# First head of clustered attention: its stack and its row of maxima written by the engines instead of by transfers

## The chip, the cores and the metric

The kernel runs on one core of a Trainium2 chip. The core has five engines that work side by side: TensorE (PE, matrix products, with weight loads as PEld), VectorE (DVE), ScalarE (ACT), GpSimd (POOL) and SyncE (SP), which here only starts transfers. Each has its own queue of instructions in a fixed order, and they wait for each other by semaphores. Matrix products land in PSUM; everything else lies in SBUF, which has 128 partitions. The metric is the device time in microseconds.

## The reference

Clustered attention over 2 batches of 8 heads, 768 positions, width 64, and then two expert layers.

```
q_assign = argmax(q_n @ c_n.T);  k_assign = argmax(k_n @ c_n.T)     # 16 clusters a head
mask   = q_assign[..., :, None] == k_assign[..., None, :]
scores = where(mask, q @ k.T / 8, -1e9)
attn   = softmax(scores);  x = attn @ v            # x: 1536 x 512
h = x @ w_in;  x = (h - tanh(h)) @ w_out           # d_ff 2048
x = (sigmoid(x @ w_gate) * (x @ w_val)) @ w_out2   # d_ff 1536
```

## The kernel before, in words

The 16 heads are worked in 8 pairs. `pair_prep(s)` prepares pair s: it loads q and k (L489, two transfers each, 192 KB a transfer), turns them on PE (L499) and copies them from PSUM with ACT into `xtq` and `xtk` (L503), 128 rows of which 64 belong to each head. DVE rounds these to a high part in `hlq` and `hlk` (L508), and POOL makes the low part (L515). PE scores all positions against the clusters (L527, 12 products); DVE makes a one-hot of the winner in five steps (L539 to L549); PE turns the one-hots (L561, six transposes); ACT scales them into `oht` (L567): -2^100 times the one-hot for q, one minus the one-hot for k.

A head's operands lie in a "stack" `stk` of four planes of 128 rows: the q and k rows in partitions 0 to 63, the 16 one-hot rows in 64 to 79, parts of the low products above, and in row 96 of plane 2 the negated row maxima. An engine writes a partition only from the same partition of its source (or, out of PSUM, from the one that PE put it in), so all stack rows are written by transfers from SBUF to SBUF (`copy`, L240), started by SP in `part` (L578).

`head_max(h)` multiplies the stack's planes 0 and 1 (L633, two products a tile of 128 positions, six tiles a head) and DVE takes each row's maximum (L637); the six columns of maxima are turned by PE (L641), copied by DVE into `mt` (L643), and written by a transfer into row 96. `head_attend(h)` multiplies the stacks again with all rows (L668, L669), ACT takes the exponential twice (L672, in f32 and f16), POOL or DVE makes the f16 remainder (L682), and PE multiplies with v (L699 to L701). v's scale for each batch comes from maxima that DVE takes over loaded parts of v (`v_part`, L436), held in buffers of kind `pt`, and from a short chain (L453 to L458). The expert layers follow (L969, L1288), with weights loaded, split and multiplied group by group.

Two things set the order. Every piece of work is a task with a priority, and `Planner.run` puts the tasks into each engine's queue before the kernel is built, from its own table of costs and from the numbers in `PRM`. And 170 tasks of two idle products each (`keep_busy`, L418), with the lowest priority, fill PE's queue wherever the planner sees it with nothing to do at the start. All 340 products are always issued.

Of the kernel before, what the change touches and what calls it, by code (L numbers as in the profile page):

```python
# [26 lines left out]
PRM = dict(  # L27
    QUEUE=2.5, AH_PE=0.15, AH_ACT=0.316, AH_DVE=0.0, AH_POOL=0.697, AH_SP=1.315, N_BUSY=170, NR=2, NRH=1,
    HX=['hx', 'hhxx'], WAR=0.797, LM=11, LV=8, ZP1=-12.75, ZP=1.744, FD=0.173, FO=0.68, LOQ=0, VHI=0, VL=6.0,
    VLS=2.185, VR=17.353, ZSV=-18.475, ZRAW=12.924, ZT=1.25, ZH=13.805, ZHL=14.25, ZS=4.5, ZC=-11.964,  # L30
    ZOT=-36.883, ZD=11.75, ZDH=6.0, ZDM=7.0, ZVL=25.5, ZVS=49.843, ZX=-0.998, ZE=34.058, ZLOW=39.356,
    ZLOWP=2.75, SEMS=1.0, TC=0.456, TW=0.74, M2=1, ZQK=0.25, ZMS=-28.375, Z0=53.342, HB=94, NB4=5, ROWS=0.0155,
    VB=9.164, RAWL=2.2, NMID=2, NPL2=2, W1L=0.7, D1L=0.322, W2L=1.623, D2L=-0.754, ZI=7.032, ZJ=1.1)


class Task:
# [168 lines left out]
def tile_cluster_attention_moe(  # L205
# [266 lines left out]
    xt_done = {}  # L472
    last = {}

    def pair_prep(s):


# [58 lines left out]
        def scores():  # L536
            return at(sm)[:, 0:G * C].rearrange("p (g c) -> p g c", c=C)
# [34 lines left out]
        for hh in range(2):  # L572
            sk = Slot("stk")
            hd = 2 * s + hh
            stk[hd] = sk
            r = hh * D

            def part(n, f, dep, src, take=(), sk=sk, z=z, hh=hh, more=0):  # L578
                x = add(SP, DMA_C, z + PRM["ZD"] + PRM["ZDH"] * hh + more, f, dep, take, lat=n * ROWS)
                use(src, x)  # L580
                return x

            def hi(nm, r=r):
# [5 lines left out]
            ts = [part(64, lambda sk=sk, hi=hi: copy(at(sk)[0:64, 0], hi("q")), [hi_t["q"]], hl["q"], [sk])]  # L589
            ts.append(part(128, lambda sk=sk, hi=hi: copy(  # L590
                at(sk)[0:64, 1::2], hi("k").unsqueeze(1).to_broadcast([64, 2, S])), [hi_t["k"], ts[0]], hl["k"]))
            for x in range(2):
                ts.append(part(C, lambda sk=sk, x=x, hh=hh: copy(
                    at(sk)[64:64 + C, x], at(oht)[(2 * x + hh) * C:(2 * x + hh + 1) * C]), [m6, ts[0]], oht))
            mready[hd] = list(ts)
# [5 lines left out]
            ts.append(part(64, lambda sk=sk, lo=lo: copy(at(sk)[0:64, 2], lo("q")), lo_t["q"] + ts[:1], hl["q"], more=PRM["ZDM"]))  # L601
# [19 lines left out]
    def head_max(h):  # L621
# [863 lines left out]
```

## Time and profile before

| | |
|---|---|
| median of 3 timed runs | 801.94 us (801.39 to 802.08) |
| profiled execution, its own time | 801.26 us |
| its span | 799.3 us |
| PE busy | 779.2 us, 97% |
| DVE busy | 573.3 us, 72% |
| ACT busy | 439.4 us, 55% |
| POOL busy | 567.3 us, 71% |
| mean granted clock of PE | 0.993 |

Busy time of PE includes the idle products of L418. An engine with a low share is not the bound of the whole, but it can be the bound of a stage; so the stages at the start are read one by one below. The granted clock is 1.00 at 2.4 GHz and 0.50 at 1.2 GHz.

### The profile page before, as it was taken

The page shows a single profiled execution, that of the slowest core. Times are in us where ns is not written, and L with a number is a line of the kernel's source. Part 1 is how long each engine was busy: PE and PEld are TensorE (multiplying, and loading weights), DVE is VectorE, ACT ScalarE, POOL GpSimd, SP SyncE. Part 2 cuts the span into 40 slices and gives each one's busy share as a digit, 9 for nine tenths or more (in the row PEclk, how much of TensorE's full clock was granted, in tenths as well). Part 3 has the DMA queues.
Part 4 walks back from the last instruction along what each step waited for, and adds up shares of the span by engine and source line. Part 5 has one row for each costly group of instructions (what it writes and reads, how often), then busy time and mean ns, then how long its engine had stood idle before and what let it go on. Part 6 is the DMA issues. An engine that isn't in the chain of part 4 may idle for free.

```text
span 799.3 us, 15929 instructions
## 1 busy us (share of the span) xinstructions
PE 779.2 (97%) x5979; PEld 731.4 (92%) x5979; DVE 573.3 (72%) x1076; ACT 439.4 (55%) x852; POOL 567.3 (71%) x597
## 2 busy tenths in 40 slices
PE   8989999999899999999999999999999999999998
PEld 8879898888779998999999999998998999999996
DVE  4887887797997866987676686998267676676434
ACT  4176778878778635554445445646552625445240
POOL 4266778776879896788688787989495766757231
PEclk9998999999999999999999999999999999999999
DMA  8866665566353100321121232122112222121004
GB/s 189 209 175 134 146 159 123 132 152 154 89 148 113 62 1 1 107 93 56 57 100 41 66 93 80 64 80 84 38 53 80 80 79 80 44 84 46 0 1 159
DMA packets 69341, 72.95 MB, mean 91 GB/s; under 512 B 30256, under 2 KB 52880, under 8 KB 69264
## 3 DMA queue, kind: packets, MB, share of 16 engines
q1 hardware_dynamic: 69264, 71.93, 32.7%
q8 instruction: 47, 0.77, 0.4%
q14 instruction: 30, 0.25, 0.1%
HBM read 48.27 MB, written 3.15 MB: 64 GB/s over the span
## 4 chain that ended last, share of the span: by engine, by line
PE 77%; DVE 10%; POOL 3%; issue 3%; DMA 3%; ACT 2%; SPq 1%; DVEq 0%; POOLq 0%; ACTq 0%
PE over_left L969 16%; PE over_left L1288 14%; PE sm L1288 11%; PE sm L969 9%; PE over_right L969 5%; PE over_right L1288 4%; DVE finr L637 2%; PE sm L418 2%; PE sm L699 2%; PE sm L700 2%; PE sm L701 2%; PE bb L633 1%; DVE vs L614 1%; PE ba L668 1%; PE bc L633 1%
## 5 line engine op out<-in xcount | busy, mean ns | idle before, releaser
L682 POOL TENSOR_TENSOR pt<-pf,pt 128x768 f16<-128x768 f32 x45 | 77.5, 1736 | 34.3 <-ACT pt L672 18.5
L682 POOL TENSOR_TENSOR ptt<-pf,ptt 128x768 f16<-128x768 f32 x34 | 58.2, 1717 | 19.7 <-ACT ptt L672 15.6
L996 POOL TENSOR_TENSOR stk<-pf,hlq 128x384 fp32r<-128x384 f32 x25 | 26.1, 1045 | 33.2 <-ACT hlq L995 33.2
L637 DVE TENSOR_REDUCE finr<-bc 128x1 fp32r<-128x768 f32 x35 | 33.2, 950 | 15.6 <-PE bc L633 13.4
L699 PE MATMUL sm<-vs,pt 128*128 128x65 f16 x330 | 43.7, 196 | 0.4 <-DVE mt L643 0.4
L700 PE MATMUL sm<-vs,pt 128*128 128x64 f16 x330 | 43.3, 197 | 0.0
L701 PE MATMUL sm<-vs,pt 128*128 128x65 f16 x330 | 43.0, 193 | 0.0
L969 PE MATMUL over_left<-stk,w 128*128 128x384 f32 x158 | 40.1, 335 | 0.0
L1288 PE MATMUL over_left<-xh,stk 128*128 128x384 f32 x132 | 40.0, 335 | 0.0
L637 DVE TENSOR_REDUCE finr<-bb 128x1 fp32r<-128x768 f32 x35 | 33.2, 949 | 7.6 <-PE bb L633 7.5
L995 ACT ACTIVATE stk<-pf 128x384 fp32r<-128x384 f32 x41 | 21.4, 523 | 30.5 <-POOL pf L1318 11.6
L699 PEld LDWEIGHTS <-pt 128*128 128x128 f16 x330 | 31.2, 97 | 6.2 <-issue 6.0
L672 ACT ACTIVATE pf<-ba 128x768 f32<-128x768 f32 x35 | 28.8, 823 | 13.3 <-PE ba L669 11.4
L1308 DVE TENSOR_TENSOR pf<-over_left,pf 128x384 f32<-128x384 f32 x32 | 17.7, 553 | 25.2 <-ACT pf L1304 11.4
L969 PE MATMUL over_left<-w,stk 128*128 128x512 f32 x118 | 34.9, 392 | 0.0
L700 PE MATMUL sm<-vs,ptt 128*128 128x64 f16 x246 | 34.8, 197 | 0.0
L699 PE MATMUL sm<-vs,ptt 128*128 128x65 f16 x246 | 34.7, 195 | 0.0
L701 PE MATMUL sm<-vs,ptt 128*128 128x65 f16 x246 | 34.4, 194 | 0.0
L672 ACT ACTIVATE pf<-bc 128x768 f32<-128x768 f32 x30 | 24.8, 826 | 14.9 <-PE bc L669 12.4
L996 POOL TENSOR_TENSOR oht<-pf,stk 128x384 fp32r<-128x384 f32 x25 | 25.6, 1025 | 9.9 <-ACT stk L995 9.2
L700 PEld LDWEIGHTS <-pt 128*128 128x128 f16 x330 | 31.5, 98 | 0.6 <-issue 0.5
L701 PEld LDWEIGHTS <-pt 128*128 128x128 f16 x330 | 31.7, 100 | 0.0
(570 smaller groups left out, 3166.8 us busy)
## 6 DMA issues: line engine op xcount, KB each, us to landing
vs<-in_moe_w_out_dram SPq DMA_DIRECT2D x48, 256.0 KB, 2.4
stk<-hlq SPq DMA_DIRECT2D x32, 192.0 KB, 2.7
stk<-hlk SPq DMA_DIRECT2D x16, 384.0 KB, 5.4
vs<-in_moe_w_in_dram SPq DMA_DIRECT2D x24, 256.0 KB, 2.6
vs<-in_moe_w_gate_dram SPq DMA_DIRECT2D x24, 256.0 KB, 2.7
vs<-in_moe_w_val_dram SPq DMA_DIRECT2D x24, 256.0 KB
rawq<-in_q_dram SPq DMA_DIRECT2D x16, 192.0 KB, 4.9
rawk<-in_k_dram SPq DMA_DIRECT2D x16, 192.0 KB, 4.6
```

The lines of the kernel that those rows point to most:

```text
L418: nc.tensor.matmul(tiles["sm", 1][:, 0:P], busy, busy, start=True, stop=True)
L637: rd.append(use(mx, add(DVE, c_dve(S), z + t, lambda t=t, mx=mx: nc.vector.tensor_reduce(at(mh)[:, t:t + 1], at(mx)[:, :, 0:HALF], axis=AX ...
L672: nc.scalar.activation(o.rearrange("p (j n) -> p j n", j=2), at(st)[:, :, 0:HALF], AF.Exp, scale=scale)
L682: lambda nce=nc.vector if on_v else nc.gpsimd, pf=pf, pt=pt: nce.tensor_tensor(at(pt)[:, 1], at(pf), at(pt)[:, 0], op=ALU.subtract), [e0, e1])
L699: nc.tensor.matmul(oview()[:, t], ph, vv[:, 0:D + 1], start=(kt == 0), stop=False)
L700: nc.tensor.matmul(oview()[:, t, 0:D], ph, vv[:, D + 1:2 * D + 1], start=False, stop=False)
L701: nc.tensor.matmul(oview()[:, t], plo, vv[:, 0:D + 1], start=False, stop=(kt == T - 1))
L969: nc.tensor.matmul(ps, a, b, start=(i == 0), stop=(i == n - 1))
L995: a = add(ACT, c_acts(CH), z, lambda: nc.scalar.activation(hi(), src(), AF.Copy), deps, take)
L996: b = add(POOL, c_pool(CH), z, lambda: nc.gpsimd.tensor_tensor(lo(), src(), hi(), op=ALU.subtract), [a])
L1288: nc.tensor.matmul(at(bank[to])[:, 0:CH], lh, rh, start=start and i == 0, stop=stop and i == 3 * KH - 1, skip_group_check=True)
L1308: return use(x, use(bank[n], add(DVE, c_dve(CH), rank[0], lambda: nc.vector.tensor_tensor(at(x), ps(n), at(x), op=ALU.add), deps)))
```

## The change

For head 0 alone, six transfers go: q and k rows, the two times 16 one-hot rows, the low q rows and the row of maxima. ACT copies q and k from `xtq` and `xtk` straight into partitions 0 to 63 of the stack, since head 0's rows lie there already. The one-hots of pair 0 are written into a zeroed buffer `pad` (one of kind `pt`) at a column offset, so that a transpose of 80 columns puts the wanted 16 rows in PSUM partitions 64 to 79; ACT (for q) and DVE (for k) scale them from there into the stack. The maxima of head 0 are written into the same buffer behind 96 zero columns, so that a transpose of 97 columns puts a tile's maxima in PSUM partition 96; ACT copies that row into the stack, in two halves. The banks' release (`ramp`) follows the new tasks. Of `PRM` four numbers differ.

```diff
-    VLS=2.185, VR=17.353, ...
+    VLS=2.185, VR=15.055, ...
-    VB=9.164, RAWL=2.2, ... W2L=1.623, ...
+    VB=9.164, RAWL=2.354, ... W2L=1.842, ... ZL0=1.3, ...
...
+    t_pad = use(pad, add(DVE, 0.9, -40, lambda: nc.vector.memset(at(pad).bitcast(F32), 0.0), take=[pad]))
+    def first_stack(sk, xts, ev, m4, z):
+        ts = []
+        for x, nm in enumerate("qk"):
+            ts.append(use(xts[nm], add(ACT, c_act(S), z + PRM["ZL0"], lambda x=x, nm=nm: nc.scalar.activation(
+                at(sk)[0:64, x], at(xts[nm])[0:64], AF.Copy), ev[nm] + ts[:1], [sk] if x == 0 else [])))
+        for x in range(2):
+            sm = Slot("smr")
+            def rows_t(x=x, sm=sm):
+                for t in range(T):
+                    nc.tensor.transpose(at(sm).bitcast(BF16)[0:64 + C, t * P:(t + 1) * P],
+                                        pad_oh()[:, t, 2 * C * x:2 * C * x + 64 + C], ident16)
+            a = use(pad, add(PE, 0.5, z + PRM["ZOT"] - 1 + 0.1 * x, rows_t, [m4], [sm]))
+            src = lambda sm=sm: at(sm).bitcast(BF16)[64:64 + C, 0:S]
+            if x == 0:
+                b = add(ACT, c_act(S) + 0.1, z + PRM["ZOT"] - 1, lambda src=src: nc.scalar.activation(
+                    at(sk)[64:64 + C, 0], src(), AF.Copy, scale=-BIG), [a, ts[0]])
+            else:
+                b = add(DVE, c_dve(S), z + PRM["ZOT"] - 1, lambda src=src: nc.vector.tensor_scalar(
+                    at(sk)[64:64 + C, 1], src(), -1.0, 1.0, op0=ALU.mult, op1=ALU.add), [a, ts[0]])
...
+            if hd == 0:
+                ts = first_stack(sk, xts, ev, m4, z)
+                ts.append(use(xts["k"], add(ACT, c_act(S), z + PRM["ZL0"] + 6, lambda sk=sk: nc.scalar.activation(
+                    at(sk)[0:64, 3], at(xts["k"])[0:64], AF.Copy), ts[:1])))
+                ts.append(add(ACT, c_act(S), z + PRM["ZL0"] + 6, lambda sk=sk: nc.scalar.activation(
+                    at(sk)[0:64, 2], at(hl["q"])[0:64, 1], AF.Copy), lo_t["q"] + ts[:1]))
+                mready[hd] = ts[:4]
...
+        if h == 0:
+            out_t = []
+            for half in range(2):
+                sm = Slot("smr")
+                def tr(half=half, sm=sm):
+                    for j in range(3):
+                        t = 3 * half + j
+                        nc.tensor.transpose(at(sm)[0:97, j * P:(j + 1) * P], pad_max()[:, t:t + 97], ident)
+                c = use(mh, add(PE, 0.33, z + T + PRM["ZMS"], tr, rd, [sm]))
+                out_t.append(use(sm, add(ACT, c_act(HALF), z + T + PRM["ZMS"], lambda half=half, sm=sm: nc.scalar.activation(
+                    at(sk)[96:97, 2, half * HALF:(half + 1) * HALF], at(sm)[96:97, 0:HALF], AF.Copy), [c])))
+            ramp.extend(out_t)
+            return out_t
```

The planner then orders everything anew. Lines of the new kernel are shifted: L499 becomes L537, L527 L565, L561 L611, L633 L697, L637 L701, L539 to L549 L577 to L599.

SP's queue at the start, before; `stk_86` is the stack of head 0, `stk_87` of head 1, `pt` holds parts of v, and the second rawk is that of pair 1:

```order
L434 DMA pt_96<-in_v_dram 128x2x384
L434 DMA pt_97<-in_v_dram 128x2x384
L489 DMA rawq_120<-in_q_dram 128x6x64 x2
L240 DMA stk_86<-hlq_122 64x768
L489 DMA rawk_123<-in_k_dram 128x6x64 x2
L240 DMA stk_87<-hlq_122 64x768
L240 DMA stk_86<-hlk_125 64x2x768
```

And now:

```order
L434 DMA pt_97<-in_v_dram 128x2x384
L527 DMA rawq_120<-in_q_dram 128x6x64 x2
L527 DMA rawk_123<-in_k_dram 128x6x64 x2
L240 DMA stk_87<-hlq_122 64x768
L240 DMA stk_86<-hlq_122 32x768
L240 DMA stk_86<-hlk_125 32x768
```

One v load and head 0's transfer of q rows no longer stand ahead of pair 1's k load.

DVE's queue in the middle of the start, around the maxima chain of pair 2, before; `finr_113` holds the maxima of head 2 and `finr_114` those of head 3, `ptt` and `pt` parts of v, `mm` the pair's cluster maxima:

```order
L637 TENSOR_REDUCE finr_113<-bc_620 128x1
L539 TENSOR_REDUCE mm_126<-sm_71 128x24
L614 SCALAR_TENSOR_TENSOR vs_89<-rawv_92,sv,vs_89 128x6x64
L643 CAST mt_115<-sm_72 6x128
L541 TENSOR_TENSOR sm_71<-sm_71,mm_126 128x384
L436 TENSOR_REDUCE vm<-ptt_104 128x1
L543 TENSOR_TENSOR sm_71<-sm_71,first 128x384
L637 TENSOR_REDUCE finr_114<-bb_80 128x1
```

And now, where `finr_114` is head 2's:

```order
L701 TENSOR_REDUCE finr_114<-bc_621 128x1
L674 SCALAR_TENSOR_TENSOR vs_89<-rawv_92,sv,vs_89 128x6x64 x2
L436 TENSOR_REDUCE vm<-ptt_104 128x1
L722 CAST mt_116<-sm_71 6x128
L436 TENSOR_REDUCE vm<-ptt_105 128x1
L436 TENSOR_REDUCE vm<-ptt_106 128x1
L577 TENSOR_REDUCE mm_126<-sm_72 128x24
L453 TENSOR_REDUCE vm<-vm 128x1
L579 TENSOR_TENSOR sm_72<-sm_72,mm_126 128x384
```

Three reductions of v now stand in one piece ahead of pair 2's chain, and head 3's maxima behind it.

PE's queue between pair 1's k transposes and the first maximum of head 0, now (`pt_96` is `pad`, `ba_76` the first bank of maxima):

```order
L537 MATMUL smr_84<-ident,rawk_123 128x128 x3
L537 MATMUL smr_85<-ident,rawk_123 128x128 x3
L498 MATMUL sm_71<-ident_141,pt_96 80x128
L498 MATMUL smr_84<-ident_141,pt_96 80x128
L611 MATMUL smr_85<-ident_141,pt_96 64x128
L565 MATMUL sm_71<-cb,xtq_121 128x96
L697 MATMUL ba_76<-stk_86 128x384 x2
```

The one-hot transposes of pair 0 (six of each kind) stand behind pair 1's k transposes; before, L561 stood ahead of them.

## Rows read from the trace of the kernel before

**Rows 1.** The page: span, and busy time, share and instructions of each engine.

```profile
span 799.3 us, 15929 instructions
PE 779.2 (97%) x5979; PEld 731.4 (92%) x5979; DVE 573.3 (72%) x1076; ACT 439.4 (55%) x852; POOL 567.3 (71%) x597
```

**Rows 2.** Windows: length; busy PE, PEld, DVE, ACT, POOL; granted clock; DMA share, GB/s.

```profile
10.00:20.00 10.00, 8.74 (x117) 8.24 (x117) 5.00 (x8) 2.73 (x5) 2.02 (x3) 1.00 0.99 177
...
50.00:60.00 10.00, 7.60 (x38) 5.48 (x37) 9.84 (x15) 6.56 (x9) 5.03 (x4) 0.85 0.70 187
60.00:70.00 10.00, 10.00 (x130) 8.92 (x129) 7.93 (x14) 5.32 (x8) 7.49 (x5) 0.64 0.83 164
...
80.00:90.00 10.00, 8.43 (x73) 7.79 (x72) 8.41 (x14) 7.66 (x12) 6.04 (x4) 1.00 0.82 166
```

**Rows 3.** The chain that ended last, 9 to 24: start, us, what.

```profile
10.47 7.62 DMA rawk<-in_k_dram
```

**Rows 4.** Timeline of PE, 15 to 47: start, us, instructions, [idle before, releaser].

```profile
15.91 0.52 PE L561 MATMUL smr<-ident,oh 128*64 128x128 bf16 x6
16.37 0.96 PE L418 MATMUL sm<-busy 128*128 128x128 bf16 x14
18.22 0.52 PE L499 MATMUL smr<-ident,rawk 128*128 128x128 f32 x3 [0.90 <-DMA rawk<-in_k_dram]
18.57 0.49 PE L499 MATMUL sm<-ident,rawk 128*128 128x128 f32 x3
...
19.91 0.41 PE L527 MATMUL smr<-cb,xtq 128*128 128x96 f32 x2
...
22.56 0.60 PE L633 MATMUL ba<-stk 80*128 80x384 f32 x2
22.99 0.52 PE L633 MATMUL bb<-stk 80*128 80x384 f32 x2
...
36.94 0.42 PE L668 MATMUL bc<-stk 112*128 112x384 f32 x1
...
46.74 0.36 PE L527 MATMUL sm<-cb,xtq 128*128 128x96 f32 x2
```

**Rows 5.** Timeline of PE, 52 to 59.

```profile
52.78 0.51 PE L633 MATMUL bb<-stk 80*128 80x384 f32 x2
53.71 0.62 PE L633 MATMUL ba<-stk 80*128 80x384 f32 x2 [0.41 <-ACT ptt L672]
55.11 0.45 PE L668 MATMUL bc<-stk 112*128 112x384 f32 x1 [0.79 <-ACT pt L672]
...
56.77 0.80 PE L633 MATMUL bb<-stk 80*128 80x384 f32 x2 [0.67 <-DVE finr L637]
58.09 0.69 PE L668 MATMUL ba<-stk 112*128 112x384 f32 x1 [0.53 <-DVE finr L637]
```

**Rows 6.** Windows around the low clock, columns as in rows 2.

```profile
53.50:57.00 3.50, 1.84 (x7) 1.19 (x8) 3.50 (x7) 2.37 (x5) 1.65 (x1) 1.00 0.36 99
...
58.50:67.00 8.50, 8.50 (x83) 7.22 (x83) 6.67 (x11) 4.45 (x7) 5.91 (x5) 0.50 1.04 219
```

**Rows 7.** Timeline of ACT, 14 to 39.

```profile
14.52 0.87 ACT L503 ACTIVATE xtq<-smr 128x384 f32<-128x384 f32 x2 [5.45 <-PE smr L499]
...
30.00 0.99 ACT L567 ACTIVATE oht<-smr,row_b,row_w 64x768 fp32r<-64x768 bf16 x1 [10.30 <-PE smr L561]
...
37.93 0.81 ACT L672 ACTIVATE pf<-bc 128x768 f32<-128x768 f32 x1 [0.89 <-PE bc L669]
```

**Rows 8.** Timeline of DVE, 11 to 23.

```profile
11.49 0.95 DVE L436 TENSOR_REDUCE vm<-pt 128x1 f32<-128x768 f32 x1 [0.15 <-DMA pt<-in_v_dram]
...
22.88 0.56 DVE L539 TENSOR_REDUCE mm<-smr 128x24 f32<-128x384 f32 x1 [7.59 <-PE smr L527]
```

**Rows 9.** Chain, 46 to 60, and DMA issues, 0 to 70 (KB, us to landing).

```profile
47.14 4.70 DMA stk<-oht
...
stk<-hlk SPq DMA_DIRECT2D x5, 384.0 KB, 6.6
```

More of the change, by code (lines that the diff above doesn't have):

```diff
@@ L29 @@
     HX=['hx', 'hhxx'], WAR=0.797, LM=11, LV=8, ZP1=-12.75, ZP=1.744, FD=0.173, FO=0.68, LOQ=0, VHI=0, VL=6.0,
[L30 removed]
+    VLS=2.185, VR=15.055, ZSV=-18.475, ZRAW=12.924, ZT=1.25, ZH=13.805, ZHL=14.25, ZS=4.5, ZC=-11.964,
     ZOT=-36.883, ZD=11.75, ZDH=6.0, ZDM=7.0, ZVL=25.5, ZVS=49.843, ZX=-0.998, ZE=34.058, ZLOW=39.356,
     ZLOWP=2.75, SEMS=1.0, TC=0.456, TW=0.74, M2=1, ZQK=0.25, ZMS=-28.375, Z0=53.342, HB=94, NB4=5, ROWS=0.0155,
[L33 removed]
+    VB=9.164, RAWL=2.354, NMID=2, NPL2=2, W1L=0.7, D1L=0.322, W2L=1.842, D2L=-0.754, ZI=7.032, ZL0=1.3, ZJ=1.1)
 class Task:
@@ L473, in tile_cluster_attention_moe, with pad_oh, pad_max @@
     last = {}
+    pad = Slot("pt")
+    def pad_oh():
+        return at(pad).bitcast(BF16).rearrange("p a n -> p (a n)")[:, 0:T * P].rearrange("p (t c) -> p t c", c=P)
+    def pad_max():
+        return at(pad).bitcast(F32).rearrange("p a n -> p (a n)")[:, T * P // 2:T * P // 2 + 96 + T]
+    t_pad = use(pad, add(DVE, 0.9, -40, lambda: nc.vector.memset(at(pad).bitcast(F32), 0.0), take=[pad]))
[18 more added lines that the diff above has]
+                    at(sk)[64:64 + C, 1], src(), -1.0, 1.0, op0=ALU.mult, op1=ALU.add), [a, ts[0]])
+            ts.append(use(sm, b))
+            ramp.append(b)
+        return ts
     def pair_prep(s):
@@ L546, in pair_prep, with oh_v @@
             at(mm)[:, 1, :, 0], scores(), axis=AX.X, op=ALU.max), [m2])
+        if s == 0:
+            oh = pad
+        def oh_v(t):
+            return pad_oh()[:, t, 2 * D - 4 * C:] if s == 0 else at(oh)[:, t].rearrange("p x h c -> p (x h c)")
         def onehot():
+            if s == 0:
+                nc.vector.tensor_tensor(
+                    pad_oh()[:, :, 2 * D - 4 * C:].rearrange("p t (g c) -> p t g c", c=C),
+                    scores().rearrange("p (t g) c -> p t g c", t=T),
+                    at(mm)[:, 1].rearrange("p (t g) c -> p t g c", t=T).to_broadcast([P, T, G // T, C]), op=ALU.is_equal)
+                return
             nc.vector.tensor_tensor(at(oh).rearrange("p t x h c -> p (t x h) c"), scores(),
                                     at(mm)[:, 1].to_broadcast([P, G, C]), op=ALU.is_equal)
-        m4 = add(DVE, c_dve(G * C), z + PRM["ZC"] + 1, onehot, [m3], [oh])
+        m4 = add(DVE, c_dve(G * C), z + PRM["ZC"] + 1, onehot, [m3, t_pad] if s == 0 else [m3], [] if s == 0 else [oh])
         use(sm, m4)
@@ L587, in lo @@
                 return at(hl[nm])[r:r + 64, 1]
[L589 to L595, printed above, removed]
+            if hd == 0:
[4 more added lines that the diff above has]
+                    at(sk)[0:64, 2], at(hl["q"])[0:64, 1], AF.Copy), lo_t["q"] + ts[:1]))
+                use(hl["q"], ts[-1])
+                mready[hd] = ts[:4]
+            else:
+                ts = [part(64, lambda sk=sk, hi=hi: copy(at(sk)[0:64, 0], hi("q")), [hi_t["q"]], hl["q"], [sk])]
+                ts.append(part(128, lambda sk=sk, hi=hi: copy(
+                    at(sk)[0:64, 1::2], hi("k").unsqueeze(1).to_broadcast([64, 2, S])), [hi_t["k"], ts[0]], hl["k"]))
+                for x in range(2):
+                    ts.append(part(C, lambda sk=sk, x=x, hh=hh: copy(
+                        at(sk)[64:64 + C, x], at(oht)[(2 * x + hh) * C:(2 * x + hh + 1) * C]), [m6, ts[0]], oht))
+                mready[hd] = list(ts)
             for w, top in ((0, 64 + C), (1, 64)):
@@ L600, in pair_prep @@
                     at(sk)[top:top + 32, 2 * w + 1], lo("k")[32 * w:32 * w + 32]), lo_t["k"] + ts[:1], hl["k"], more=PRM["ZDM"]))
-            ts.append(part(64, lambda sk=sk, lo=lo: copy(at(sk)[0:64, 2], lo("q")), lo_t["q"] + ts[:1], hl["q"], more=PRM["ZDM"]))
+            if hd:
+                ts.append(part(64, lambda sk=sk, lo=lo: copy(at(sk)[0:64, 2], lo("q")), lo_t["q"] + ts[:1], hl["q"], more=PRM["ZDM"]))
             mrow[hd] = ts
@@ L625, in head_max, with mh_v @@
         sk = stk[h]
-        mh, mt, sm = Slot("finr"), Slot("mt"), Slot("smr" if h < NRH else "sm")
+        mh, mt, sm = pad if h == 0 else Slot("finr"), Slot("mt"), Slot("smr" if h < NRH else "sm")
         rd = []
+        def mh_v(t):
+            return pad_max()[:, 96 + t:97 + t] if h == 0 else at(mh)[:, t:t + 1]
         for t in range(T):
@@ L637, in head_max @@
             rd.append(use(mx, add(DVE, c_dve(S), z + t, lambda t=t, mx=mx: nc.vector.tensor_reduce(
-                at(mh)[:, t:t + 1], at(mx)[:, :, 0:HALF], axis=AX.XY, op=ALU.max, negate=True),
-                [a] + rd[:1], [mh] if t == 0 else [])))
+                mh_v(t), at(mx)[:, :, 0:HALF], axis=AX.XY, op=ALU.max, negate=True),
+                [a] + rd[:1], [mh] if t == 0 and h else [])))
         last["max"] = last.get("max", []) + rd
+        if h == 0:
[11 more added lines that the diff above has]
+            return out_t
         c = use(mh, add(PE, 0.11, z + T + PRM["ZMS"], lambda: nc.tensor.transpose(
```

3 lines of the change are left out of this document (1 added, 2 removed).

## The prediction, made before the changed kernel was run

> **What bounds the kernel now.** I read the page first. The span is 799.3 us and TensorE (PE) is busy 97% of it [rows 1], so a change at the start is worth something only where PE stood still, worked on nothing useful, or ran at the lower clock. Next the windows of ten microseconds [rows 2]: there the reader sees one bad place in the first 100 us. In 50 to 60 PE is busy 7.60 of 10 us and the granted clock is 0.85; in 60 to 70 PE is full but the clock is 0.64; in 80 to 90 PE is busy 8.43. Everywhere else before 100 PE is nearly full at 1.00. In 10 to 20, where the change sits, PE is busy 8.74.
>
> Then the chain and the timeline of PE for the start. The first maximum of head 0 (L633) starts at 22.56, directly behind the twelve score matmuls of pair 1, which begin at 19.91; these wait for pair 1's k transposes at 18.22, and those for their load, with 0.90 us of idle [rows 3, 4]. So it is not the stack of head 0 that ends last there: the raw k load of the next pair does. From there to 46.74, where pair 2's scores begin, PE never waits: whatever it has no work for is filled with the 340 idle matmuls of L418 [rows 4]. All 340 are in both kernels, so PE cannot gain from work that comes earlier in this stretch; only its waits could go, of which the longest behind the first microsecond is that 0.90.
>
> The bad place is read from the timeline behind 52: four waits of 0.41, 0.79, 0.67 and 0.53 us, mostly for VectorE (DVE) and the exponentials, 2.40 together [rows 5]. In 53.5 to 57 PE is busy 1.84 of 3.50 us; behind that the granted clock is 0.50 (1.2 GHz) in 58.5 to 67 with PE full [rows 6]. Those 8.5 us of full work at half rate lose 4.3 us. The hole costs 2.40 + 4.3 = 6.7 us in all.
>
> **The change, part by part.** I sum against the profiled execution, 801.26 us (span 799.3 and 1.96 around it); the median of the three timed runs, 801.94, is 0.68 above it, within their own spread of 0.69.
>
> *Removed.* Six transfers into head 0's tile (q rows, k rows twice, two one-hot rows, low q, maxima: 192 + 384 + 2 x 48 + 192 + 3 KB, about 0.87 MB) and the DVE copy of the maxima. SyncE (SP) reaches the loads of pair 1 sooner: of what stands ahead of its k load, a v load of 384 KB and the hlq transfer of 192 KB are gone. The load landed at 10.47 + 7.62 = 18.1 [rows 3]. Around it the DMA moved 177 GB/s with its engines full [rows 2]; 0.58 MB are 3.2 us by that, and nothing if the small transfers behind the load slow it as much. I take 1.9, nearer to the row: it lands at 16.2.
>
> *Added on PE.* Twelve one-hot transposes: six take 16.37 - 15.91 = 0.46 [rows 4], so 0.9. Six f32 transposes of the padded maxima in place of one: three take 18.57 - 18.22 = 0.35 [rows 4], so 0.7, less 0.1 for the old one. Together **+1.5 us**, which no filler gives back, since its number is fixed.
>
> *Added elsewhere.* Seven more ScalarE (ACT) instructions: four f32 copies of 768 columns at about 0.8 (the exponentials of that width take 0.81), the one-hot row like L567 at 0.99, two maxima rows of 384 columns, up to 0.44 each (two evictions of that width take 0.87) [rows 7]. ACT idles 5.45 us before 14.52 and 10.30 before 30.00 [rows 7], which covers them; without that cover they would cost their 5.1 us. DVE gets one 768-column one-hot operation, about 0.95, and one memset of about that; it idled 7.59 before 22.88 [rows 8], so nothing.
>
> *Moved on PE.* The transposes of head 0's one-hots now stand behind pair 1's k transposes, so behind its load. From 16.2 on: k transposes 0.7, three groups of six 0.46 each with waits for the bank copies, then ACT's one-hot row 0.99, and the scores start near 18.75. They take 22.56 - 19.91 = 2.65, so head 0's first maximum starts near 21.4 instead of 22.56. Adding filler and maxima at 0.43 (22.99 - 22.56) in the new order, the first attend matmul comes at about 34.7 instead of 36.94 [rows 4]. Pair 2's scores come near 48.6 instead of 46.74, with all six maxima of head 2 done instead of three. Three of them are 1.3 us of PE: in work done PE is level or up to 0.6 behind. The wait for the k load changes little, since the filler ahead of it ends earlier too: **-0.2** (between -0.9, all gone, and +1.7, the load no earlier and the one-hot transposes behind it).
>
> *The hole.* In the new order DVE does three reductions of v (L436, 0.95 each) in one piece ahead of the maxima chain of pair 2, and head 3's k rows are queued on SP behind a raw k load that waits for PE's last transposes of pair 2. Walking through with the durations of [rows 8]: DVE issues pair 2's one-hot near 57.5; head 3's k and one-hot rows land near 56 (issue near 49.6 for 384 KB, 6.6 us [rows 9]), where they let its first maximum start at 52.78 before [rows 5]. PE then waits some 0.6 + 1.0 + 0.9 + 0.5 = 3.0 us between 55 and 62. That is no less idle than the 2.40 of before, so I expect the clock to fall again, but some 3 us later and up to the same 67, with about 5.2 us of full work in it: 2.6 lost. 3.0 + 2.6 against 6.7: **-1.1** (bounds -6.7, no hole, and +3.4, below).
>
> *Behind it.* By about 62 DVE has done some 4 us more than before (two more v reductions, one more low part, both casts of pair 2) and one attend tile of head 2 is through. From about 102 us of before on, PE has the same order in both kernels through the rest of the attention but its last tiles, so the lead at that point is what the end sees. The idle of 1.57 in 80 to 90 [rows 2] hangs on the exponentials and the v scaling of that stage, which one attend tile (two exponentials of 0.81 [rows 7]) and the DVE lead bring forward by about as much: **-1.7** with a little from behind it (bounds 0 and -3.7).
>
> The planner number for late weights (W2L) only puts four loads of w_gate and w_val ahead of the last four of the first layer's w_out, far from the start. With PE busy 97% over the span [rows 1] I cost it at 0, bounds -0.5 and +1.
>
> Sum: 1.5 - 0.2 - 1.1 - 1.7 = -1.5, so 801.26 - 1.5 = **799.8 us**.
>
> **A rule weighed.** Two serial transfers leave the path from one-hot and maxima to the next matmul; a pair of one-hot transfers of a later pair took 4.70 us in the chain [rows 9]. The Trainium skill, DMA: Bandwidth & Descriptors, section Anatomy of one DMA, puts a fixed cost of about 2 us on a transfer whatever its size (stated for the path that GpSimd starts; these start on SP); two of them would be 4 us by that. That the start runs on filler [rows 4] speaks against seeing it whole at the end; no run here isolates such a transfer yet.
>
> **The rivals.**
> 1. *The hole closes.* With head 2's maxima done early PE stays busy enough and the clock never leaves 1.00. For: the three maxima and 2.6 us of DVE work are out of the way. Against: the v reductions put in front. The hole then costs 0 to 3.0 us: 1.5 - 0.2 - 6.7 to -3.7 - 1.7, so 794.2 to 797.2.
> 2. *Nothing comes through.* The filler is fixed, the hole costs the same 6.7, and the idle at 80 to 90 stays or partly goes: +1.5 - 0.2 and 0 to -1.3, so 801.3 to 802.6. For: PE-bound from 18 to 52 in both. Against: DVE's lead. No change.
> 3. *The hole grows: slower.* Head 3's k rows, queued behind the waiting raw load, land another 2 us late; PE idles 5.0, and the lower clock then covers 10.2 us of the dense attend-times-v work: 5.1 lost. 5.0 + 5.1 - 6.7 = +3.4, with +1.5, -0.2 and nothing behind: +4.7, so 806.0. It decides if head 3's first maximum starts later than about 58. For: SP stands still for that load. Against: DMA is nearly empty by then.
> 4. *The whole path comes through.* Two removed transfers at 2.35 us (half of 4.70 [rows 9]) shift everything behind the ramp, by 4.7, less the 1.5 of transposes: 3.2, so 798.1. Against: PE's unbroken row of fillers [rows 4].
>
> **How the numbers follow.** Forecast 0.38, rival 1 0.20, rival 2 0.24, rival 3 0.13, rival 4 0.05. A measurement can tell about 0.2%, 1.6 us: faster means under 800.3, slower over 803.5. Of the forecast three quarters lie under 800.3 (0.29), with rivals 1 and 4 that is 0.54. The rest of it and most of rival 2 are no change: 0.29. Rival 3 and the upper edge of rival 2 are 0.17. The forecast's own range is 798.0 to 801.4. The wide one runs from inside rival 1 (795.0) to past rival 2 (803.5), which leaves out the far part of rivals 1 and 3.
>
> **What would show it.** In the changed profile: pair 1's k load landing near 16.2; head 0's first maximum near 21.4 and the first attend near 34.7; pair 2's scores near 48.6; PE waits of about 3 us between 55 and 62 and a granted clock of 0.5 ending near 67; less than 0.5 us of idle where before had 1.57. I am wrong if the clock stays at 1.00 (rival 1), if head 3's first maximum starts behind 58 (rival 3), or if PE waits grow behind 102, where its order is unchanged.

## The result, and the profile after

Every time is in us, of one core. Four executions of the changed kernel took 806.74 to 808.10, median 807.9, beside 802.01 for the kernel before: ratio 1.0065, 95% interval 1.0046 to 1.0084. Slower by 0.65%, where I had forecast 799.8 and a range up to 803.5. With more executions (below) the ratio is 1.0058 (1.0037 to 1.008).

The page of the changed kernel: span, then busy time of each engine. Its profiled execution took 808.1.

```profile
span 806.3 us, 15961 instructions
PE 783.8 (97%) x5996; PEld 734.4 (91%) x5996; DVE 579.9 (72%) x1077; ACT 444.8 (55%) x859; POOL 566.1 (70%) x597
```

PE is busy 4.6 us more than before [rows 1], where I had counted 1.5 of new work (work at half clock counts double), and the span is 7.0 longer. The timeline of PE, against [rows 4, 5]; the lines lie lower in the changed file: L537 is L499 of before, L565 L527, L697 L633, L747 L668, L611 L561:

```profile
15.40 0.82 PE L537 MATMUL smr<-ident,rawk 128*128 128x128 f32 x6
...
17.90 0.41 PE L565 MATMUL sm<-cb,xtq 128*128 128x96 f32 x2
...
20.55 0.60 PE L697 MATMUL ba<-stk 80*128 80x384 f32 x2
...
33.76 0.42 PE L747 MATMUL ba<-stk 112*128 112x384 f32 x1
...
48.16 0.41 PE L565 MATMUL sm<-cb,xtq 128*128 128x96 f32 x2
...
55.61 0.62 PE L697 MATMUL bc<-stk 80*128 80x384 f32 x2
56.65 0.52 PE L611 MATMUL sm<-ident,oh 128*64 128x128 bf16 x6 [0.42 <-DVE oh L599]
...
59.23 1.01 PE L697 MATMUL ba<-stk 80*128 80x384 f32 x2 [0.83 <-ACT pt L751]
...
63.33 0.69 PE L747 MATMUL ba<-stk 112*128 112x384 f32 x1 [0.82 <-DVE finr L701]
...
206.75 0.44 PE L747 MATMUL bc<-stk 112*128 112x384 f32 x1 [1.29 <-DVE finr L701]
...
208.98 1.01 PE L697 MATMUL bb<-stk 80*128 80x384 f32 x2 [1.26 <-DVE finr L701]
```

The wait for pair 1's k load (0.90) is gone; head 0's first maximum starts at 20.55 instead of 22.56, the first attend matmul at 33.76 instead of 36.94, pair 2's scores at 48.16, head 3's first maximum at 55.61. The hole between 55 and 64 is still there. The windows (columns as in [rows 2]):

```profile
10.00:20.00 10.00, 9.91 (x115) 9.45 (x115) 5.42 (x8) 5.44 (x9) 2.33 (x3) 1.00 0.77 174
50.00:60.00 10.00, 8.48 (x50) 6.44 (x48) 9.70 (x19) 8.76 (x13) 5.53 (x4) 0.88 0.69 170
60.00:70.00 10.00, 9.18 (x122) 7.99 (x121) 7.26 (x8) 3.44 (x5) 8.50 (x7) 0.60 0.28 84
80.00:90.00 10.00, 8.90 (x76) 7.99 (x75) 8.49 (x14) 7.49 (x12) 5.30 (x4) 1.00 0.68 147
90.00:100.00 10.00, 9.55 (x159) 8.17 (x157) 8.38 (x12) 7.42 (x12) 8.53 (x7) 1.00 0.55 128
...
200.00:210.00 10.00, 7.46 (x118) 6.20 (x118) 10.00 (x10) 6.92 (x10) 9.51 (x8) 0.89 0.33 90
210.00:220.00 10.00, 10.00 (x138) 8.75 (x137) 6.13 (x15) 6.62 (x10) 6.68 (x4) 0.77 0.28 65
...
550.00:560.00 10.00, 9.04 (x42) 6.98 (x41) 7.33 (x13) 4.13 (x11) 8.08 (x10) 1.00 0.07 25
560.00:570.00 10.00, 9.13 (x46) 8.16 (x46) 5.82 (x15) 6.85 (x16) 8.27 (x10) 1.00 0.39 134
```

Two things stand out that the start has no part in: the granted clock falls a second time, at 207.9, and PE stands still 1.83 us between 550 and 570, where the trace of before has 0.36. The same windows of before:

```profile
200.00:210.00 10.00, 7.74 (x134) 6.54 (x133) 10.00 (x11) 6.94 (x11) 9.52 (x8) 1.00 0.31 83
210.00:220.00 10.00, 9.88 (x143) 8.23 (x142) 8.54 (x20) 8.16 (x14) 8.33 (x6) 1.00 0.40 96
...
550.00:560.00 10.00, 9.64 (x47) 8.24 (x46) 8.57 (x21) 6.34 (x16) 10.00 (x12) 1.00 0.48 153
560.00:570.00 10.00, 10.00 (x51) 8.75 (x50) 1.67 (x3) 4.81 (x10) 3.09 (x4) 1.00 0.11 33
```

To see where the 7 us come from I took the start of the same matmul (the n-th of its line) in both traces and subtracted. After less before:

```
at 98 us (head 5's maxima)           -0.3
at 200 us                            -0.1
at 221 us (behind the second fall)   +2.75
first expert matmul, 251 us          +3.4
expert layer 1, 274 to 471 us        +4.0 to +4.3
at 504 us                            +4.9
from 567 us to the end               +7.2
```

So in this pair the rearranged start is level with the old one; 2.85 come at 208, 1.4 in the last attention tiles (PE idle 0.62 in 245 to 250 and 0.92 in 265 to 270, by waits for DVE, where before had none; it has 0.72 in 260 to 265, against 0.40), and 3.1 in the experts.

What one pair says of the start is loose. The experiments below left more traces whose start is not edited: at 98 us the changed order stands at -0.3 (this pair), -0.1 (again), -1.0 (W2L as before), +2.6 (products ahead of 206) and -0.5 (both of these), the old order at 0 (this pair), -1.5 (W2L as changed) and +1.5 (products ahead of 206). The means are level too (+0.1 and 0.0), but a single execution is off by up to 2.5 us. In the one at +2.6 PE stood still 1.9 us ahead of a group of k transposes at 39.5 us, and the clock fell there; the others of that order have at most 0.45 of idle at that place. The later steps repeat: the last attention tiles cost 1.5 up to 274 us in all five of these traces, of which 0.3 comes back by 350.

### The profile page after: what moved, and what is told of

The parts are those of the page before. It is cut to its first block, busy times and chain, and to the rows that moved or that the text cites. A ratio compares the mean times of both kernels' runs of the same rounds, so it can differ in the third digit from the quotient of the medians.

```text
span 806.3 us, 15961 instructions
## 1 busy us (share of the span) xinstructions
PE 783.8 (97%) x5996; PEld 734.4 (91%) x5996; DVE 579.9 (72%) x1077; ACT 444.8 (55%) x859; POOL 566.1 (70%) x597
## 4 chain that ended last, share of the span: by engine, by line
PE 71%; DVE 14%; POOL 6%; issue 4%; ACT 3%; DMA 2%; SPq 0%; DVEq 0%; POOLq 0%; ACTq 0%
PE over_right L1367 12%; PE over_left L1048 9%; PE sm L1367 9%; PE over_left L1367 8%; PE sm L1048 8%; PE over_right L1048 6%; DVE finr L701 3%; PE sm L418 2%; PE sm L778 2%; PE sm L779 2%; PE sm L780 2%; PE sm L565 2%; PE ba L697 1%; PE ba L747 1%; PE bb L747 1%
## 5 line engine op out<-in xcount | busy, mean ns | idle before, releaser
L996 DVE SCALAR_TENSOR_TENSOR over_left<-vs,over_left 128x256 uint32<-128x256 uint32 x118 | 50.6, 429 | 4.0
L995 DVE TENSOR_SCALAR over_left<-vs 128x256 uint32<-128x256 uint32 x118 | 49.4, 419 | 0.1
L1074 ACT ACTIVATE stk<-pf 128x384 fp32r<-128x384 f32 x47 | 24.6, 523 | 39.4 <-POOL pf L1397 13.4
L701 DVE TENSOR_REDUCE finr<-bc 128x1 fp32r<-128x768 f32 x36 | 34.2, 949 | 14.2 <-PE bc L697 13.3
L1075 POOL TENSOR_TENSOR stk<-pf,stk 128x384 fp32r<-128x384 f32 x26 | 27.1, 1043 | 22.3 <-ACT stk L1074 22.2
L751 ACT ACTIVATE pf<-bb 128x768 f32<-128x768 f32 x38 | 31.3, 823 | 19.2 <-PE bb L748 16.8
L701 DVE TENSOR_REDUCE finr<-ba 128x1 fp32r<-128x768 f32 x34 | 32.3, 949 | 9.3 <-PE ba L697 9.3
L1367 PE MATMUL over_right<-xh,stk 128*128 128x384 f32 x110 | 33.1, 336 | 0.0
L1075 POOL TENSOR_TENSOR stk<-rawv,hlq 128x384 fp32r<-128x384 f32 x13 | 13.3, 1022 | 28.0 <-ACT hlq L1074 27.9
L997 DVE SCALAR_TENSOR_TENSOR ry<-vs,over_left 128x256 uint32<-128x256 uint32 x64 | 27.0, 421 | 7.5 <-POOL ry L1287 1.2
L1075 POOL TENSOR_TENSOR hlq<-pf,hlk 128x384 fp32r<-128x384 f32 x25 | 25.9, 1034 | 8.6 <-ACT hlk L1074 7.5
```

The source lines that it names most:

```text
L751: nc.scalar.activation(o.rearrange("p (j n) -> p j n", j=2), at(st)[:, :, 0:HALF], AF.Exp, scale=scale)
L995: nc.vector.tensor_scalar(c, high, 3, 0x3FFFFFF8, op0=ALU.logical_shift_left, op1=ALU.bitwise_and)
L996: nc.vector.scalar_tensor_tensor(c, high, 0xC0000000, c, op0=ALU.bitwise_and, op1=ALU.bitwise_or)
L997: nc.vector.scalar_tensor_tensor(at(cut), low, 29, c, op0=ALU.logical_shift_right, op1=ALU.bitwise_or)
L1075: b = add(POOL, c_pool(CH), z, lambda: nc.gpsimd.tensor_tensor(lo(), src(), hi(), op=ALU.subtract), [a])
L1367: nc.tensor.matmul(at(bank[to])[:, 0:CH], lh, rh, start=start and i == 0, stop=stop and i == 3 * KH - 1, skip_group_check=True)
```

## The experiments

In the table "old" is the kernel before, run beside each group on the same chip; n counts executions, times are medians, clock is the mean granted clock over the executions (a fall lowers it). Medians and ratio don't follow each other exactly, since the times of one program spread with the clock.

```
kernel                               n   median  old     ratio (95%)              clock  old
changed, again                       12  808.17  802.92  1.0058 (1.0037-1.0080)   0.990  0.990
changed, W2L as before               12  804.49  802.92  1.0009 (0.9988-1.0030)   0.990  0.990
before, W2L as changed               12  804.53  802.92  1.0025 (1.0003-1.0047)   0.991  0.990
changed, products ahead of 206       12  805.24  802.92  1.0025 (1.0003-1.0048)   0.994  0.990
changed, W2L, fewer idle products    12  803.18  802.02  1.0006 (0.9987-1.0025)   0.992  0.991
before, fewer idle products          12  800.59  802.02  0.9987 (0.9972-1.0002)   0.991  0.991
changed, W2L, products ahead of 206  11  802.77  802.02  1.0005 (0.9989-1.0021)   0.994  0.991
changed, all three numbers as before  4  810.03  802.02  1.0106 (1.0092-1.0121)   0.988  0.991
before, products ahead of 206        12  801.68  802.09  0.9987 (0.9973-1.0001)   0.993  0.991
before, both small edits             12  801.18  802.09  0.9975 (0.9959-0.9990)   0.992  0.991
changed, W2L, both small edits       12  800.96  802.09  0.9979 (0.9965-0.9993)   0.994  0.991
changed, W2L, products in the hole   12  805.01  802.09  1.0025 (1.0007-1.0043)   0.991  0.991
```

**The changed kernel again.** No edit.

> The changed kernel once more, nothing edited, as the base of the others. Theory A (the second fall of the clock, at 208 us, belongs to this order of work): the granted clock of the span is 0.989 again in most executions, the time 807.5 to 808.2, ratio to the kernel before 1.0075. Rival B (that fall is chance, one execution in so many): some executions at 0.994 and near 805, and the kernel before shows it at times as well, near 804.5.

The clock was 0.989 in 8 of 12 executions, 0.987 in one and 0.991 to 0.994 in three; so theory A for the most part. But the kernel before had a mean of 0.990 on this chip too, and rival B holds in its second half. In the profiled execution of this run the second fall came in 170 to 180 and not behind 205; in that of the kernel before with fewer idle products (below) there is one in both. The windows of the two, in this order:

```profile
170.00:180.00 10.00, 8.95 (x119) 8.01 (x120) 8.69 (x12) 6.50 (x10) 7.21 (x6) 0.83 0.43 110
205.00:215.00 10.00, 7.45 (x101) 6.17 (x100) 9.79 (x15) 6.17 (x10) 8.64 (x7) 1.00 0.50 122
```

```profile
170.00:180.00 10.00, 9.24 (x120) 8.46 (x121) 8.63 (x12) 7.07 (x11) 8.14 (x6) 0.83 0.47 113
205.00:215.00 10.00, 7.75 (x85) 6.35 (x84) 9.77 (x15) 5.10 (x9) 7.34 (x6) 0.83 0.55 135
```

So the second fall is not tied to the change: both orders have stalls in which the clock may or may not fall. In the trace of this run, without a fall there, the changed order loses 0.3 in the stall at 208; so 2.5 of the 2.85 in the first pair are a matter of which executions were caught. Whether the changed order loses its clock more often is open: on this chip 3 of its 24 executions (this run and the next one) have a clock of 0.993 or more, and 10 of 35 of the kernel before.

**The order of the late weights, both ways.**

```diff
-W2L=1.842        (changed kernel)      -W2L=1.623        (kernel before)
+W2L=1.623                              +W2L=1.842
```

> The changed kernel with the planner number for late weights W2L put back from 1.842 to 1.623, which changes the order of the expert layers alone. Theory A (that order makes PE wait at 500 and between 550 and 570, where it fell 0.95 and 2.2 us behind): 3.1 us less, 804.4 to 805.2. Rival B (the delay in the experts is carried there from the start, by engines that are late, and the order of weights costs nothing, as I forecast): 807.5 to 808.2.

> The kernel before with W2L alone set to the new 1.842; nothing of the first head is touched. Theory A: it loses the same 3.1 us, 804.7 to 805.4 against 801.9, by waits of PE at 500 and between 550 and 570. Rival B (the order of weights costs nothing): 801.4 to 802.4.

The changed kernel gains 3.7 by the medians (0.49 points of ratio, and the two intervals do not overlap) and is then level with the kernel before. The kernel before loses 1.6 by the medians, half of what theory A says; the interval, 0.2 to 3.8 us, would by itself hardly part the theories. At an equal clock of 0.993 or more it takes 803.6 (6 executions) against 801.2 (10) on the same chip, so 2.4 more, and by the trace it loses 2.75 (its distance to the unedited kernel grows by 0.55 around 500 and by 2.1 from 538 to 567). Theory A on both sides, a little under its size in the old order. The waits of PE between 480 and 590 (engine, line, waited for; us, times, longest), first in the changed kernel, then with W2L as before, then in the kernel before with the new W2L (L1288 and L969 there are L1367 and L1048 here):

```profile
PE over_left L1367 <- ACT rawv L1383: 0.9, 1, 0.9
PE over_right L1048 <- ACT pf L1335: 0.8, 1, 0.8
PE over_right L1367 <- ACT pf L1383: 0.5, 1, 0.5
```

```profile
PE over_right L1367 <- ACT rawv L1383: 0.5, 1, 0.5
```

```profile
PE over_left L1288 <- ACT pf L1304: 1.1, 2, 0.9
PE over_left L969 <- ACT pf L1256: 0.7, 1, 0.7
```

PE does not wait for the load of a weight in any of them: it waits for what ACT reads out of PSUM. Why ACT is late stands in ACT's own queue. Two rows of the changed kernel, and the same two of the kernel before with the new W2L:

```profile
558.96 0.42 ACT L1276 ACTIVATE stk<-ry 128x256 fp32r<-128x256 f32 x1 [0.98 <-POOL ry L1287]
559.28 0.47 ACT L1335 ACTIVATE pf<-over_right 128x384 f32<-128x384 f32 x1
```

```profile
553.13 0.42 ACT L1197 ACTIVATE stk<-ry 128x256 fp32r<-128x256 f32 x1 [0.98 <-POOL ry L1208]
553.46 0.47 ACT L1256 ACTIVATE pf<-over_left 128x384 f32<-128x384 f32 x1
```

The first row of each rounds a piece of a late weight, and ACT stands still 0.98 us before it, until POOL has made a sum of such pieces. The second is the sigmoid that empties the bank for which PE waits until 559.80 (553.98). The other two waits of the changed kernel have the same kind of row ahead of them: ACT waits 0.99 at 498.68 for a weight that DVE cuts, ahead of the copy that PE waits for until 500.10, and 0.43 at 563.03, ahead of five more copies and the one that holds PE until 565.83. In the kernel before ACT has no such wait between 552 and 562. So the number moves more than loads: in `weights2` one priority, with small offsets, orders a late weight's load, its cutting on DVE, its rounding on ACT and its sums on POOL, and the planner deals PE's products out anew around them. That PE waits behind this work is read from the traces; a run with the loads moved alone was not made. The windows of the kernel before with the new W2L show the same idle place, and those of the changed kernel with the old one show most of it gone:

```profile
550.00:560.00 10.00, 8.30 (x37) 6.50 (x37) 8.35 (x21) 7.87 (x19) 10.00 (x13) 1.00 0.39 113
560.00:570.00 10.00, 10.00 (x51) 9.16 (x52) 2.21 (x4) 4.57 (x9) 4.67 (x7) 1.00 0.15 47
```

```profile
550.00:560.00 10.00, 10.00 (x48) 8.50 (x47) 8.65 (x21) 6.84 (x17) 10.00 (x12) 1.00 0.32 89
560.00:570.00 10.00, 9.46 (x51) 8.68 (x50) 4.25 (x10) 4.99 (x11) 4.43 (x5) 1.00 0.34 97
```

**Idle products ahead of the wait at 206.** Behind attend-times-v tile 4 of head 10, in its own PSUM bank:

```diff
+                if (h, t) == (10, 4):
+                    for _ in range(22):
+                        nc.tensor.matmul(at(o)[:, 392:512], busy, busy[:, 0:120], start=True, stop=True)
```

> The changed kernel with 22 idle products of 0.056 us (1.2 us) behind one attend-times-v tile, just ahead of the wait of PE at 206.75 us, the order otherwise the same. Theory A (the second stretch at half clock is PE standing still there for 1.29 and 1.26 us): the granted clock stays 1.00 at 208 to 215, 2.5 to 2.9 us less, 805.0 to 805.6. Rival B (the fall at 208 has another cause than PE's idle time): the clock falls there as before and the time is 807.5 to 808.2, or up to 1 us more if the products delay the wait's end.

> The changed kernel with W2L at 1.623 and the 22 idle products ahead of the wait at 206 us, both at once. If the two effects add (3.7 by W2L and 2.9 by the products in the last call): 6.6 under the changed kernel, 801.5 when the kernel before is at 802.9, that is 1.4 under it. If they overlap (the clock falls elsewhere instead): 803 to 804.5, no better than W2L alone.

> The kernel before with the same 22 idle products ahead of its own wait at 206 us (1.00 and 1.26 us of idle there). Theory C (the stall at 206 to 209 is in both kernels, and either may lose its clock there, some executions do and some don't): its mean granted clock rises from 0.990 or 0.991 to about 0.993 and the median falls by 0.5 to 2 us. Rival A (only the changed kernel falls there): clock and time as the kernel before within 0.5 us.

Alone it is as theory A said: 2.9 under the changed kernel, no execution below 0.993. (Its profiled execution is the slowest of the twelve, 808.1 at 0.994, and the one that stands at +2.6 at 98 us; behind that it loses 0.3 at 208, as the changed kernel does without a fall.) The window of 205 to 210, of the changed kernel again, and with the products:

```profile
205.00:210.00 5.00, 2.85 (x31) 2.21 (x29) 5.00 (x5) 2.92 (x6) 5.00 (x5) 1.00 0.34 80
```

```profile
205.00:210.00 5.00, 4.87 (x72) 4.34 (x73) 5.00 (x5) 3.34 (x5) 5.00 (x4) 1.00 0.19 43
```

With W2L put back as well the two did not add up: 802.77, 0.75 above the kernel before, where 1.4 below was expected. The clock was up as hoped (0.994). Its profiled execution ends 2.0 behind the one of before: 1.5 come in the last attention tiles, and 1.0 between 538 and 567, where the run with W2L alone lost nothing. Whether that 1.0 stands in its other executions is not known, and the interval of the ratio (0.9989 to 1.0021) is as wide as the dispute. In the kernel before, whose two waits there are nearly the same,

```profile
PE ba L633 <- DVE finr L637: 1.3, 1, 1.3
PE bc L668 <- DVE finr L637: 1.0, 1, 1.0
```

the products raised the mean clock from 0.991 to 0.993 and took 0.4 off the median: theory C in kind, a little under its size. The 0.4 alone would fit rival A as well; it is the clock that parts them, and 4 of the 12 executions still had 0.991.

**Fewer idle products in the start.** The last 70 filler tasks issue one product instead of two:

```diff
-        for _ in range(2):
+        for _ in range(2 if i < 100 else 1):
```

> The changed kernel with W2L at 1.623 and 70 idle products fewer (3.9 us of PE; each of the last 70 filler tasks, from about 33 us on, issues one product instead of two), the order otherwise the same. Base: the same kernel with all products, 804.5 beside 802.9 for the kernel before, hence +1.6. Theory F (the start did gain, and the fixed filler holds it): the first maxima of pair 2 and head 3 come up to 3.9 us earlier and the difference to the kernel before falls to between -0.4 and -2.3. Rival G (DVE's maxima set the pace from 33 to 62, the filler costs nothing): PE's idle time of that stretch grows by what the products took, the difference stays at +1.0 to +2.0. Rival H: the emptier stretch lets the clock fall earlier, +2.5 to +5.

> The kernel before with the same 70 products fewer. Theory F: its start had less to give, since head 0's maxima come 2 to 3 us later there; 0 to -2 us against the kernel before, less than the changed kernel gains by the same edit. Rival G: within 1 us of the kernel before, by more idle time of PE. Rival H: +1 to +3 by an earlier fall of the clock.

By the medians the changed kernel goes from +1.6 to +1.2 against the kernel before, and the kernel before from 0 to -1.4; the intervals overlap, so the times decide neither for F nor for G. The trace speaks for a mixture: with 3.9 us taken out, the changed kernel stands at -2.5 at 98 us, where with all products and the same W2L it stood at -1.0 (-1.0 to +2.6 over the five traces above), and the rest is new idle time of PE, as its timeline shows:

```profile
40.72 0.62 PE L697 MATMUL bc<-stk 80*128 80x384 f32 x2 [0.27 <-ACT ptt L751]
42.46 0.61 PE L697 MATMUL bc<-stk 80*128 80x384 f32 x2 [0.26 <-DVE finr L701]
...
55.15 0.52 PE L611 MATMUL sm<-ident,oh 128*64 128x128 bf16 x6 [0.87 <-DVE oh L599]
```

The last of these waits is 0.42 in the changed kernel. H did not occur in the traces: the clock first fell at 58.2 and 56.6, about as before. What I had expected of the old start, that it had less to give, is open: by the medians it gained no less, but its trace stands at -0.4 at 98 us, inside the -1.5 to +1.5 that it has with all products.

**All three planner numbers as before.**

```diff
-VR=15.055  RAWL=2.354  W2L=1.842
+VR=17.353  RAWL=2.2    W2L=1.623
```

> The changed kernel with all three planner numbers (VR, RAWL, W2L) as before: the first head's new operations alone. The planner then orders the attention anew. Theory A (the first head's operations are worth about nothing at an equal clock, -0.2 up to 200 us, and the 1.4 us lost in the last attention tiles belong to the new numbers): within 1 us of the kernel before. Rival B (those 1.4 us come with any new order of the start, since the planner's clock runs on from it): +1 to +3. Rival C (the new numbers were needed for the new start): +3 to +6, by more idle time of PE between 50 and 100.

8.0 over the kernel before, worse than rival C. The planner orders the whole attention anew; its distance to the kernel before is +1.5 at 98, +10 at 206 and +12 at 274 us in the profiled execution; so little of it stands between 50 and 100, where rival C looked for it. The window of 225 to 250, here and with the new VR and RAWL:

```profile
225.00:250.00 25.00, 22.03 (x282) 19.17 (x279) 20.62 (x34) 17.59 (x29) 18.17 (x14) 0.93 0.46 126
```

```profile
225.00:250.00 25.00, 23.57 (x328) 20.08 (x329) 20.26 (x36) 22.10 (x34) 21.70 (x14) 1.00 0.45 130
```

PE waits 3.0 of 25 us and loses its clock once more. So with the first head's new operations the new VR or RAWL or both gain some 6 us (+1.6 with them, +8.0 without; they were not parted), and of the three numbers only W2L was seen to cost. The last attention tiles cost about 2 here too, by other waits, so the loss there does not hang on the new numbers alone, as theory A had it. Since every number reshuffles the order, the first head's operations alone could not be run in the old order of the rest.

**Idle products in the hole.** Twenty behind the small matmuls at 55.1:

```diff
+            for _ in range(20 if b == 1 else 0):
+                nc.tensor.matmul(at(sc)[:, 2 * P:3 * P], busy, busy, start=True, stop=True)
```

> The changed kernel with W2L at 1.623 and 20 idle products (1.1 us) behind the small matmuls at 55.1 us, in the hole between 55 and 60. Theory: if PE's idle time there brings the clock down, it stays at 1.00 in more of the executions; PE's work of 58 to 68 then runs at full rate, but DVE was busy 9.7 of 10 us in that stretch, so that most of it turns into waits: mean clock 0.992 to 0.996 against 0.990, time -1 to -2.5 against the 804.5 of the base. Rival (the hole is DVE's, a faster PE only waits longer, and the products delay the maximum behind them): clock up, time within 1 us of the base or up to 1 us above it.

The rival: mean clock 0.991 instead of 0.990, time 805.0 against 804.5; beside the kernel before of its own group, +2.9 instead of +1.6, somewhat more than the rival allows, with intervals that overlap. In the profiled execution the clock fell at 62 instead of 57, and PE waited longer for DVE's maximum, 1.63 where it had been 0.82, as its timeline shows (the edit moves the lines down by 5):

```profile
59.41 0.62 PE L702 MATMUL ba<-stk 80*128 80x384 f32 x2 [0.81 <-ACT pt L756]
63.03 0.69 PE L752 MATMUL ba<-stk 112*128 112x384 f32 x1 [1.63 <-DVE finr L706]
```

**Both small edits, on either kernel.** The products ahead of 206 and the 70 fewer in the start, together.

> The kernel before with both small edits: 70 idle products of the start fewer, and the 22 idle products ahead of the wait at 206 us. If they add: -1.4 by the first and -0.5 to -2 by the second, so 1.9 to 3.4 us under the kernel before, faster than both kernels. If the clock falls elsewhere instead: 0 to -1.5.

> The changed kernel with W2L at 1.623 and both small edits. By the profiled executions it stands 2.5 us ahead of the kernel before at 100 us, loses 1.4 in the last attention tiles and a few tenths behind: about -0.8, and the clock at 208 stays up, so 0 to -2 against the kernel before. Rival (the medians so far, +1.2 with fewer products): +0.5 to +1.5.

Both beat the kernel before and the changed one: 0.25% and 0.21% under the kernel before by the ratio (2.0 and 1.7 us; 0.9 and 1.1 by the medians), both intervals clear of 1. The first lies between its two cases, the second within its range. They differ by 0.2 us in the median: with W2L as before and the same small edits, no difference between old start and new start can be measured in the times. The two traces show one that does not last: at 206 us the new start is 2.35 ahead of the unedited kernel before and the old one level (0.0), then the new order loses 0.3 at 208 and 1.5 in the last attention tiles, and at the end they stand at -0.7 and +0.1.

## Why the prediction was wrong

**The step that failed: the planner number for late weights at 0, bounds -0.5 and +1.** It cost 3.1 in the traces of the pair, 3.0 in those of the second run, 2.75 the other way round. I wrote that the number only puts four loads ahead of four others, that these lie far from the start and that PE is busy 97% over the span [rows 1], and took an average for a stage. The runs showed in its place that the work on these weights moves with the loads: it stands in ACT's queue ahead of what empties PE's banks, and PE waits 0.54, 0.76 and 0.87 us behind it. I had not looked at a window between 480 and 570, nor at what the new number does to the engines' lists there, only at the loads. Without this step the changed kernel measures 1.0009 (0.9988 to 1.003).

**What I did not foresee behind 100 us.** I said that from 102 on PE has the same order "through the rest of the attention but its last tiles, so the lead at that point is what the end sees". The last tiles are where it was not so: about +1.5 in every variant of the changed kernel that keeps the new VR and RAWL (about 2 in the one that does not), and nothing in the kernel before with the new W2L. Which entry of the plan starts it was not tried, so its cause is open. And the clock at 208 cost the profiled pair 2.5, in a stall that stands in both traces. I summed one profiled execution of before, with a single fall; 99 executions of that kernel spread from 799.8 to 808.5: those at a clock of 0.993 or more have a median of 801.3 (40 of them), at 0.989 to 0.992 802.5 (33), below that 805.3 (26).

**The start.** Forecast -1.5, measured about -0.1 to -0.3 at 98 to 200 us in the pair and level in the mean of the traces; with their spread that is no sharp number. Term by term, from the pair alone:
- New matmuls: forecast +1.5. Read directly it is 1.4: the twelve transposes run from 16.06 to 16.98, so 0.92, the six of the maxima from 30.55 to 31.12, so 0.57, less 0.1 for the old one. The balance comes near it: idle time and clock gain 1.6 up to 100 us (PE idles 0.19 less in 0 to 10 and 0.84 less from there on, and 0.56 by the clock, below), and -0.3 comes out, which leaves 1.3.
- The k load: forecast -0.2. The wait went altogether here (0.7 of it stands in the changed kernel's second trace); 10 to 20 has 0.09 of idle instead of 1.26, but 20 to 40 has 0.58 instead of 0.06. Of that 0.45 is the idle place at 37.7, which is not in three other traces of this order. The landing was early enough for k transposes at 15.40, so 16.2 was late by 0.8 or more.
- The hole: forecast -1.1. PE idles 2.34 in 50 to 70 (1.52 and 0.82) against 2.40, and I had said 3.0. In the stretch at half clock, before and after,

```profile
57.03:67.27 10.24, 9.71 (x90) 7.93 (x90) 8.41 (x14) 5.57 (x8) 6.90 (x5) 0.50 1.03 237
```

```profile
57.68:67.92 10.24, 8.59 (x72) 6.79 (x72) 9.15 (x8) 5.65 (x8) 8.96 (x7) 0.50 0.19 55
```

  PE was busy 9.71 and 8.59, so (9.71 - 8.59) / 2 = 0.56 less is lost; with the idle time about -0.6. The fall ended at 67.9 where I had said 67, but began 0.65 later than before where I had said some 3, with 8.6 us of work in it where I had said 5.2. Rival 1 (the clock never falls) failed; rival 3's condition (head 3's first maximum behind 58) was not met at 55.61, so the slower result is not its doing, though it names the right side.
- Behind it: forecast -1.7. In 80 to 90 idle went from 1.57 to 1.10, and 90 to 100 gave 0.33 of that back (9.55 against 9.88): -0.14. I argued that this idle time hangs on DVE's lead by 62 and on one more attend tile. DVE's lead came (busy 47.2 us by 62 against 41.7, some 1.9 of it new work), the attend tile did not: PE had begun 12 attend tiles by 62 in both traces.

**Rivals 2 and 4.** Of the start alone rival 2 comes nearest: +1.5 of matmuls, and what comes through balances them. Its reason, the fixed filler, is right in part by the traces: with fewer products the new start stands at -2.5 and -2.2 at 98 us. The times do not decide it. Rival 4's path is real up to the first attend matmul (3.2 earlier), which is as far as it got; and 2.0 of the 3.2 are there at head 0's first maximum already, ahead of which PE had waited for pair 1's k load, so 1.2 come behind it. The rule I weighed there (the Trainium skill, DMA: Bandwidth & Descriptors, Anatomy of one DMA: about 2 us fixed in a transfer that GpSimd starts) would make two removed transfers some 4 us, as an estimate. No run here isolates a transfer, so none shows it.

## What to carry to other kernels

Where a change comes with new numbers for a planner, cost each number by itself, in the stage whose order it touches: here no gain of the part named in the change could be measured and the number behind it cost 3 us. A number that moves a load moves all that is done with what it loads: look for that work in the queue of the engine that frees the banks. Look at the order beyond the point where two plans seem to meet again, to the last tile. Before two profiled executions are subtracted, take more than one of each, since traces of one order were 3.6 us apart at 98 us; compare their granted clocks, and when a stall of 2 us stands in both, count the fall of the clock as something that either may have.

## What the runs showed of the hardware

Whether TensorE's clock fell in a given stall differed from execution to execution of one program: the kernel before ran at mean clocks from 0.984 to 0.994 on one chip, and the times follow, 799.9 to 808.5. In the changed kernel it fell at 207.9, behind a wait of 1.29 us and at the start of one of 1.26, in one trace; in another, with 1.28 and 1.26 at the same place, it did not, and fell at 171. Filling such a stall with 22 idle products kept all 12 executions of the changed kernel at 0.993 or above (in the old order 8 of 12) and held nothing up that the trace shows, while filling a stall in which another engine was already the bound (DVE, 9.7 of 10 us) gained no time.
